# Attention with a mixture block on one core: the global attention's division, turning and value products rewritten, and the orders of all chunks replaced

## The chip, the core and the metric

The kernel runs on one core of a Trainium2 chip. The time is the device time of that core in microseconds (us). Three runs of the kernel before took 904.52, 904.91 and 905.95, a median of 904.91. The core's engines run side by side, each with its own queue of instructions: TensorE (PE) for matrix products, with its weight loads shown apart (PEld), VectorE (DVE), ScalarE (ACT), GpSimd (POOL), and SyncE (SP), which issues the DMAs. Instructions of different engines wait for each other by semaphores.

## The reference

Eight batches, eight heads, 512 local and 32 global tokens of 64 dimensions each. Global tokens attend to all 544 keys, local tokens to the 32 global keys and to a window of 32 keys on each side. The attention's rows then go through a normalised, gated pair of products (512 to 1536 to 512).

```
k_all = concat([k_g, k_l], axis=2); v_all = concat([v_g, v_l], axis=2)
out_g = sm(scale * q_g @ k_all.T) @ v_all            # 32 x 544 scores per head
s_ll  = where(|i - j| <= 32, scale * q_l @ k_l.T, -1e9)
out_l = sm(concat([scale * q_l @ k_g.T, s_ll])) @ v_all
x     = concat([out_g, out_l]) as (8 * 544) x 512    # B*S rows, H*D columns
xn    = x / sqrt(mean(x * x) + 1e-6) * rms_g
g, val = xn @ w_gate, xn @ w_val
out   = (g * sigmoid(g) * val) @ w_out
sm(s): e = exp(s - max(s)); e / (sum(e) + 1e-9)
```

The change concerns the line of `out_g`, and the order of everything that runs beside it.

## The kernel before

**Chunks.** The rows are worked in nine chunks. Chunks 0 to 7 are the 512 local tokens of one batch each, chunk 8 the 256 global tokens of all batches. A chunk is first attended (its scores, softmax and values), then normalised and split into f16 parts, and then sent through the gated products, which are most of PE's work: f16 products such as `pq<-xh,wt`, `pr<-wu,hs` and `po<-wo,h`. While the products of chunk c run, the attention of chunk c+1 and the first of chunk c+2 are done between them.

**Orders.** The function that builds the program records, for chunks 1 to 8, each step's instructions under a name. A table of names per chunk, `_ORDER_1` to `_ORDER_8`, then says in which order they are issued. All engines follow this order. Because the recorded calls are all played back in one place, nearly every instruction in the profile has the same line, L1929, and one tells them apart by their tiles. A name is a step and a part of it: `P5.0` and `R5.0` are the products of the fifth piece of work and what follows them on the other engines, `w`, `t`, `n` and `O` are weight fetches, the remainders of a piece of work, normalisation and output products. Names with a slash belong to attention: `S/0+1.0` is the step S (scores) of unit 0 of the next chunk, part 0. Chunk 0 is issued by another table that the change leaves as it is.

**Local attention.** A chunk from 2 to 7 has two local units (`local_halves`), of four heads each. Their steps are the loads L and V, scores S, the softmax in pieces M, N, E and F, the division D, the turn T on DVE (`STREAM_TRANSPOSE et<-e`: each 32x32 block is transposed in place), and the value products A and B (tile `a`), which add up 32 keys at a time, with the keys of four groups of 32 partitions. `A` holds the first part of the blocks and `B` the rest, so a unit's values are issued in one piece if B stands right behind A in the table, and in two otherwise. X and Y copy the result out of PSUM.

**Global attention.** `global_unit(b)` does the 32 global queries of batch b: eight heads as two halves h of four strips p of 32 partitions. There are eight such units; one falls into each of the tables 1 to 6 and two into table 7. Its steps:

- `GL`, `GV`: the loads of queries and keys (`gkq`, two tiles) and of the values (`gv`, three tiles). The values lie as five groups of 112 keys (the last of 96), the keys on the partitions.
- `GS`: sixteen score products into four PSUM banks.
- `GM`, `GN`: for each half the least score by DVE, the exponential with its sum by ACT, and, after the second, the sum's reciprocal on DVE.
- `GT` (`transp`): ten f32 transposes on PE into three PSUM banks (`gt`), and three copies by ACT to the tile `gpt`.
- `GA` (`values`): for each half, group of keys and strip one product, 40 in all, into one PSUM bank (`ga`). The turned exponentials (up to 112 keys x 32 queries) are the stationary side, 64 columns of values move.
- `GD` (`divide`): DVE multiplies the 128x128 result by the reciprocals (`gx`).
- `GX` (`turn`): one more f32 transpose on PE, and a copy by ACT into `xg`, where the global tokens of all batches gather for chunk 8.

**PSUM.** The four banks with the tag `pa`, given out in turn by `attn_bank`, serve the attention of both kinds: local scores and values, global scores, transposes and values, and some turns of the normalisation. A bank is free again when its last reader is done.

Of the kernel before, what the change touches and what calls it, by code (L numbers as in the profile page):

```python
# [9 lines left out]
F32 = mybir.dt.float32  # L10
# [12 lines left out]
P = 128  # L23
# [43 lines left out]
w1.0 w0.0 S/0+1.0 P8.0 P9.0 N1/0+1.0 N2/0+1.0 N0/0+1.0 N3/0+1.0 w2.0 M1/0+1.0 M2/0+1.0 E2/0+1.0 w3.0  # L67
M0/0+1.0 w5.0 P0.0 R9.0 F2/0+1.0 M3/0+1.0 R10.0 P4.0 P5.0 D2/0+1.0 w6.0 E3/0+1.0 F3/0+1.0 D3/0+1.0
D2/0+1.1 E0/0+1.0 F0/0+1.0 D3/0+1.1 D0/0+1.0 P1.0 R1.0 P10.0 T2/0+1.0 R2.0 GL/1+1.0 L/2+1.0 R5.0
R6.0 P6.0 P7.0 P11.0 D0/0+1.1 R7.0 E1/0+1.0 F1/0+1.0 D1/0+1.0 D1/0+1.1 P12.0 T3/0+1.0 T0/0+1.0 P2.0  # L70
P3.0 T1/0+1.0 w8.0 w9.0 A/0+1.0 B/0+1.0 X/0+1.0 R8.0 R11.0 P13.0 R12.0 R13.1 P16.0 R3.0 P14.0 P15.0
w12.0 w14.0 X/0+1.1 w15.0 R9.1 R4.0 V/2+1.0 R5.1 R13.0 R14.0 w42.0 Y/0+1.1 Y/0+1.0 w18.0 w20.0 R15.0
P24.0 P17.0 R17.0 R18.0 P25.0 R25.0 GS/1+1.0 P22.0 P23.0 GM/1+1.0 w21.0 w23.0 GM/1+1.1 GN/1+1.0
R26.0 w46.1 P26.0 P27.0 GN/1+1.1 GT/1+1.0 X/0+1.2 GT/1+1.1 R27.0 R28.0 w24.0 P20.0 R29.1 GT/1+1.2
GT/1+1.3 P21.0 R21.0 w26.0 R22.0 w17.0 P18.0 w27.0 GN/1+1.2 R16.0 R23.0 R24.0 P19.0 R25.1 R19.0
R20.0 S/2+1.0 M0/2+1.0 P32.0 M2/2+1.0 N3/2+1.0 GV/1+1.0 E2/2+1.0 M3/2+1.0 E3/2+1.0 N0/2+1.0 w48.1
M1/2+1.0 w44.0 N2/2+1.0 E1/2+1.0 w29.0 P33.0 R33.0 R34.0 N1/2+1.0 w30.0 R17.1 P28.0 P34.0 P35.0
# [12 lines left out]
R65.0 GX/1+1.0 R65.1 P57.0 n64.0 P58.0 P59.0 n61.0 D3/0+2.0 D3/0+2.1 n63.0 T1/0+2.0 w11.0 R59.0  # L90
R59.1 GX/1+1.1 n65.1 n66.0 T2/0+2.0 T0/0+2.0 T3/0+2.0 n65.0 n62.1 n63.1
# [16 lines left out]
T1/2+1.0 P41.0 F0/2+1.0 D0/2+1.0 R34.1 t36.0 GX/1+1.1 D2/2+1.1 T2/2+1.0 D0/2+1.1 t36.1 T0/2+1.0
R39.0 R40.0 t31.1 R41.0 t42.0 t37.1 A/2+1.0 B/2+1.0 X/2+1.0 Y/2+1.0 t37.0 X/2+1.1 Y/2+1.1 P50.0
# [2058 lines left out]
```

## Time and profile before

| | |
|---|---|
| median of three runs | 904.91 us |
| the profiled execution's own time | 906.6 us |
| its span in the trace | 904.8 us |
| MATMUL rows on PE, weight loads | 11430, 11430 |
| instructions on DVE, ACT, POOL | 1831, 1341, 244 |
| bytes moved by DMA | 212.03 MB in 101007 packets |

The profile is of one execution. Its span is the time from the first to the last instruction that it shows. Busy times are given by engine, and a group's row gives the number of instructions of one kind, their busy time and the mean time of one. PE's rows overlap, since a product streams in while the one ahead of it drains: what a product costs PE is read from the start of one row to the start of the next. An f32 product stands as two rows.

### The profile page before, as it was taken

The page shows a single profiled execution, that of the slowest core. Times are in us where ns is not written, and L with a number is a line of the kernel's source. Part 1 is how long each engine was busy: PE and PEld are TensorE (multiplying, and loading weights), DVE is VectorE, ACT ScalarE, POOL GpSimd, SP SyncE. Part 2 cuts the span into 40 slices and gives each one's busy share as a digit, 9 for nine tenths or more (in the row PEclk, how much of TensorE's full clock was granted, in tenths as well). Part 3 has the DMA queues.
Part 4 walks back from the last instruction along what each step waited for, and adds up shares of the span by engine and source line. Part 5 has one row for each costly group of instructions (what it writes and reads, how often), then busy time and mean ns, then how long its engine had stood idle before and what let it go on. Part 6 is the DMA issues. An engine that isn't in the chain of part 4 may idle for free. (4 is left out here: it accounts for less than half of the span.)

```text
span 904.8 us, 27760 instructions
## 1 busy us (share of the span) xinstructions
PE 867.7 (96%) x11430; PEld 667.4 (74%) x11430; DVE 725.8 (80%) x1831; ACT 555.3 (61%) x1341; POOL 277.2 (31%) x244
## 2 busy tenths in 40 slices
PE   6699979999999998999999999999999999999998
PEld 4544445545547885588888888888888888888887
DVE  6899998988787687878987888789877886787554
ACT  6899997547354666357665856668565852456232
POOL 0000000033335676515521344223521453134311
PEclk9699999999999999999999999999999999999999
DMA  9983625499277786698778777777876666888675
GB/s 331 406 288 126 196 69 171 153 290 305 75 216 254 224 266 205 195 318 248 222 268 272 247 225 254 267 234 252 282 244 206 227 206 211 261 245 274 218 244 181
DMA packets 101007, 212.03 MB, mean 234 GB/s; under 512 B 8081, under 2 KB 34449, under 8 KB 100881
## 3 DMA queue, kind: packets, MB, share of 16 engines
q1 hardware_dynamic: 100448, 209.94, 70.7%
q8 instruction: 89, 1.46, 0.7%
q10 hardware_dynamic: 432, 0.33, 0.1%
q14 instruction: 38, 0.30, 0.1%
HBM read 183.24 MB, written 27.00 MB: 232 GB/s over the span
## 5 line engine op out<-in xcount | busy, mean ns | idle before, releaser
L1929 PEld LDWEIGHTS <-wt 128*128 128x128 f16 x3312 | 321.6, 98 | 46.3 <-issue 7.0
L1929 PE MATMUL pq<-xh,wt 128*128 128x256 f16 x1152 | 204.0, 273 | 1.3 <-DVE s L1929 1.3
L1929 PE MATMUL pq<-ht,wt 128*128 128x256 f16 x1296 | 156.4, 273 | 1.9 <-DVE v L1929 1.3
L1929 PE MATMUL pq<-xl,wt 128*128 128x256 f16 x576 | 157.0, 273 | 0.0
L1929 ACT ACTIVATE e<-e,sm 128x128 f32<-128x128 f32 x288 | 104.3, 390 | 8.4 <-DVE sm L1929 8.4
L1929 POOL TENSOR_TENSOR e<-e,sm 128x512 f32<-128x512 f32 x24 | 29.2, 1225 | 217.2 <-DVE sm L1929 211.0
L1929 PE MATMUL pr<-wu,hs 128*128 128x256 f16 x792 | 92.6, 273 | 1.2 <-DMA wu<-wb 1.2
L1929 POOL TENSOR_TENSOR hs<-u,hs 128x512 f16<-128x512 f32 x50 | 61.1, 1236 | 97.1 <-ACT hs L1929 92.1
L1929 POOL TENSOR_TENSOR hu<-v,hu 128x256 f16<-128x256 f32 (+1 forms) x60 | 57.1, 966 | 106.3 <-ACT hu L1929 93.0
L1929 PEld LDWEIGHTS <-hs 128*128 128x128 f16 x792 | 77.3, 98 | 10.7 <-issue 1.8
L1929 PE MATMUL pr<-wu,hu 128*128 128x256 f16 x594 | 70.2, 273 | 0.6 <-ACT os L1929 0.6
L1929 ACT ACTIVATE t<-u,half_inv 128x512 f32<-128x512 f32 x72 | 50.3, 718 | 30.9 <-DVE u L1929 29.2
L1929 DVE TENSOR_TENSOR v<-pq,s 128x512 f32<-128x512 f32 x72 | 49.3, 685 | 20.3 <-PE pq L1929 17.4
L1929 PEld LDWEIGHTS <-hu 128*128 128x128 f16 x594 | 57.9, 98 | 7.6 <-issue 0.9
L1929 PE MATMUL po<-wo,h 128*128 128x512 f16 x288 | 63.6, 379 | 0.0
L1651 PE MATMUL p<-xh,wf 128*128 128x512 f16 x192 | 58.8, 379 | 3.4 <-DVE t L1763 1.5
L1929 DVE TENSOR_TENSOR s<-pq,s 128x512 f32<-128x512 f32 x66 | 44.5, 684 | 20.2 <-ACT s L1929 11.2
L1929 ACT COPY s<-pq 128x512 f32<-128x512 f32 x72 | 41.4, 582 | 30.7 <-PE pq L1929 22.2
L1929 DVE SCALAR_TENSOR_TENSOR t<-t,u 128x512 f32<-128x512 f32 x72 | 54.8, 768 | 5.1 <-ACT t L1929 4.9
L1929 PE MATMUL p<-xh,wf 128*128 128x512 f16 x192 | 58.6, 379 | 0.0
L1651 PEld LDWEIGHTS <-wf 128*128 128x128 f16 x288 | 27.7, 98 | 38.2 <-issue 4.4
L1929 ACT COPY u<-pq 128x512 f32<-128x512 f32 x36 | 21.0, 583 | 51.7 <-PE pq L1929 50.9
(380 smaller groups left out, 1704.3 us busy)
## 6 DMA issues: line engine op xcount, KB each, us to landing
wt<-wd SPq DMA_DIRECT2D x120, 512.0 KB, 5.8
wu<-wb SPq DMA_DIRECT2D x36, 512.0 KB, 5.9
wr<-in_w_in_dram SPq DMA_DIRECT2D x24, 512.0 KB, 8.9
wu<-wa SPq DMA_DIRECT2D x24, 512.0 KB, 4.6
k<-in_qkb_dram SPq DMA_DIRECT2D x24, 448.0 KB, 7.1
gkq<-in_gkq_dram SPq DMA_DIRECT2D x16, 576.0 KB, 7.5
wt<-wd SPq DMA_DIRECT2D x36, 256.0 KB, 4.4
v<-in_vb_dram SPq DMA_DIRECT2D x24, 352.0 KB, 5.6
```

The costliest lines, as they stand in the source:

```text
L1651: nc.tensor.matmul(ps[:, :n], rows[:, a, o : o + P], ch[z][k][:, :n], start=(k == 0 and i == 0), stop=(k == NK - 1 and i == 2),)
L1929: return lambda *a, **k: write(self.engine, lambda: call(*a, **k))
```

## The change

Four things are changed in the global unit, and all eight tables are replaced by others.

- **Division.** ACT multiplies the exponentials by the reciprocals, a half at a time (128x544), ahead of the turn. `GD` is gone.
- **Turning.** DVE transposes each half in 32x32 blocks (`STREAM_TRANSPOSE`, 128x544) into `gpt`. The ten PE transposes and ACT's three copies are gone.
- **Values.** The values lie in DRAM as 17 blocks of 32 keys, four strips of 32 partitions, 128 columns (two heads of 64). A product takes 32 keys on one strip: stationary are the 128 columns of v, and 64 columns move (32 queries of each half). 17 blocks by four strips are 68 products, and each strip has a PSUM bank of its own. The result is already turned, with the dimensions on the partitions; of its four quadrants the two on the diagonal are used (64x32 each). `gv` is loaded as two tiles, of nine and eight blocks.
- **Taking.** Eight copies of 64x32 bring the result from the four banks into `xg`, four on ACT and four on DVE. The PE transpose `gx` and the copy behind it are gone.

```diff
         def load_v(i):
             t = pool.tile([P, 1152], F32, tag="st", bufs=ST, name=f"gv{b}{i}")
-            n = min(1024, 5 * 512 - i * 1024)
-            nc.sync.dma_start(t[:GC, :n], gv[b, :, i * 1024 : i * 1024 + n])
-            st["v"] += [t[:, j * 512 : (j + 1) * 512] for j in range(n // 512)]
+            m0, n = ((0, 9), (9, 8))[i]
+            nc.sync.dma_start(t[:, : n * P], gv[b, :, m0 * P : (m0 + n) * P])
+            st["v"] += [t[:, m * P : (m + 1) * P] for m in range(n)]
...
-        def transp():
+        def turn():
             e = st["e"]
...
+            pt = pool.tile([P, 1280], F32, tag="gpt", bufs=1, name=f"gpt{b}")[:, : 2 * NG]
+            st["pt"] = pt.rearrange("p (h n) -> p h n", h=2)
             for h in range(2):
...
-                    nc.tensor.transpose(o, e[:, h, c * GC : c * GC + n], ident)
...
+                nc.scalar.mul(e[:, h, :], e[:, h, :], st["sm"][:, h, 3:4])
+            for h in range(2):
+                nc.vector.transpose(st["pt"][:, h, :], e[:, h, :])
 
         def values():
...
+            ps = st["a"] = [attn_bank(f"ga{b}{p}") for p in range(4)]
+            for m in range(NG // SG):
+                for p in range(4):
+                    r = slice(p * SG, (p + 1) * SG)
+                    nc.tensor.matmul(
+                        ps[p][:, : 2 * SG].rearrange("p (h q) -> p h q", h=2),
+                        st["v"][m][r, :],
+                        st["pt"][r, :, m * SG : (m + 1) * SG],
+                        start=(m == 0),
+                        stop=(m == NG // SG - 1),
+                        skip_group_check=True,
+                    )
+
+        def take():
+            for p in range(4):
+                for h in range(2):
+                    d = slice(h * D, (h + 1) * D)
+                    x, a = xg[d, p, b * SG : (b + 1) * SG], st["a"][p][d, h * SG : (h + 1) * SG]
+                    if p % 2 == 0:
+                        nc.scalar.copy(x, a)
+                    else:
+                        nc.vector.tensor_copy(x, a)
...
-            ("GV", lambda: [load_v(i) for i in (1, 2)], 0, [("GS", 1)]),
+            ("GV", lambda: load_v(1), 0, [("GS", 1)]),
...
-            ("GT", transp, 1, [("GN", GG[1] - 2)]),
-            ("GA", values, 1, [("GT", GG[2])]),
-            ("GD", divide, 0, [("GA", 1)]),
-            ("GX", turn, 1, [("GD", GG[3] - 1)]),
+            ("GT", turn, 0, [("GN", 1)]),
+            ("GA", values, 1, [("GT", GG[1] + GG[2] - 3)]),
+            ("GX", take, 0, [("GA", 1)]),
```

Of the tables, the first lines of `_ORDER_2`:

```diff
-P1.0 R1.0 P2.0 P4.0 R2.0 R4.0 w0.0 w4.0 GL/1+1.0 w2.0 P0.0 R0.0 R2.1 w4.1 w5.0 A/0+1.0 P3.0 P5.0
-R3.0 R5.0 R6.1 R6.0 P6.0 R6.2 t8.0 t9.0 t10.0 B/0+1.0 X/0+1.1 P7.0 R7.0 X/0+1.0 Y/0+1.1 P9.0 Y/0+1.0
+GL/1+1.0 w4.0 P0.0 R0.0 A/0+1.0 B/0+1.0 Y/0+1.1 X/0+1.0 P1.0 R1.0 w0.0 w2.0 w4.1 P2.0 P4.0 R4.0 R2.0
+P5.0 R2.1 L/2+1.0 R5.0 X/0+1.1 P7.0 R6.1 R6.0 t7.0 w5.0 P8.0 w9.0 R7.0 w11.1 Y/0+1.0 w13.1 w14.0
```

What this moves, at three places. The rows give the line, the operation, the tiles (out<-in, with the program's numbers) and the shape; L1929 of before is L1910 of after, and a LDWEIGHTS row is a weight load.

First PE, while the products of chunk 3 run, at the global unit of batch 2. Before, the ten transposes stand between two f16 products:

```order
L1929 MATMUL pq6_1_2610<-ht37_2564,wt3_13_2596 128x256
L1929 MATMUL gt20_2627<-ident_70,ge2_2600 112x128 x4
L1929 MATMUL gt2_2626<-ident_70,ge2_2600 96x128
L1929 MATMUL gt21_2628<-ident_70,ge2_2600 112x128 x4
L1929 MATMUL gt2_2626<-ident_70,ge2_2600 96x128
L1929 LDWEIGHTS wt3_20_2598
L1929 MATMUL pq6_2_2635<-ht36_2558,wt3_20_2598 128x256
```

and its values further on, as the first half's three rows, which the second half repeats:

```order
L1929 MATMUL pq6_3_2661<-ht37_2564,wt3_33_2652 128x256
L1929 MATMUL ga2_2638<-gv20_2585,gpt2_2625 32x64 x8
L1929 MATMUL ga2_2638<-gv21_2605,gpt2_2625 32x64 x8
L1929 MATMUL ga2_2638<-gv22_2606,gpt2_2625 32x64 x4
```

Now the transposes are gone, and the values are four banks in turn, 68 products in one go (the first round and the end of the last one):

```order
L1910 MATMUL pq5_4_2675<-xh35_2555,wt3_41_2651 128x256
L1910 MATMUL ga20_2628<-gpt2_2609,gv20_2579 128x64
L1910 MATMUL ga21_2629<-gpt2_2609,gv20_2579 128x64
L1910 MATMUL ga22_2630<-gpt2_2609,gv20_2579 128x64
L1910 MATMUL ga23_2631<-gpt2_2609,gv20_2579 128x64
L1910 MATMUL ga20_2628<-gpt2_2609,gv20_2579 128x64
```

```order
L1910 MATMUL ga22_2630<-gpt2_2609,gv21_2599 128x64
L1910 MATMUL ga23_2631<-gpt2_2609,gv21_2599 128x64
L1910 LDWEIGHTS wt3_41_2651
L1910 MATMUL pq6_4_2670<-ht37_2558,wt3_41_2651 128x256
```

The values stand a little later among the pieces of work than before (between the products of piece 41 of the chunk, against piece 33), and they write four banks where they wrote one.

Second DVE at the same unit. Before, the division of the result stood among the rows of the gated products (`u`, `v`) and the local turns (`et`):

```order
L1929 TENSOR_TENSOR u_4_2688<-pq5_4_2684,s6_4_2680 128x2x256
L1929 TENSOR_TENSOR gx2_2642<-ga2_2638,gsm2_2599 128x128
L1929 TENSOR_TENSOR v_4_2686<-pq6_4_2679,s1_4_2682 128x2x256
```

Now the turn of the exponentials stands well ahead of the values:

```order
L1910 RECIPROCAL sm9_2636<-sm9_2636 128x4
L1910 STREAM_TRANSPOSE gpt2_2609<-ge2_2594 128x544 x2
L1910 TENSOR_TENSOR v_3_2661<-pq6_3_2652,s1_3_2656 128x2x256
```

and the four copies of the result stand three rows behind the first of the piece of work (`s1_4`) whose products run right before the values on PE:

```order
L1910 TENSOR_TENSOR s1_4_2673<-pq5_4_2675,s1_4_2673 128x512
L1910 TENSOR_TENSOR s6_4_2671<-pq1_4_2672,s6_4_2671 128x512
L1910 STREAM_TRANSPOSE et90_2641<-e901_2660 128x512
L1910 COPY xg_77<-ga23_2631 64x32 x2
L1910 COPY xg_77<-ga21_2629 64x32 x2
L1910 SCALAR_TENSOR_TENSOR t6_2667<-t6_2667,u_3_2663 128x512
```

DVE's one row of 128x128 has become two turns ahead of PE's values and four small copies behind them.

Third PE, while the products of chunk 2 run, at the values of a local unit (tile `a7`). Before, they are one piece:

```order
L1929 MATMUL a73_2518<-et70_2470,v70_2441 64x96
L1929 MATMUL a73_2518<-et71_2471,v71_2442 64x96
L1929 MATMUL a70_2515<-et70_2470,v70_2441 64x96
L1929 MATMUL a70_2515<-et71_2471,v71_2442 64x96
```

Now the first part and the second are apart, with f16 products between them:

```order
L1910 MATMUL a73_2512<-et70_2465,v70_2438 64x96
L1910 MATMUL a73_2512<-et71_2466,v71_2439 64x96
L1910 LDWEIGHTS wt2_42_2475
L1910 MATMUL pq5_4_2494<-xh23_2386,wt2_42_2475 128x256
```

The same holds for three of the twelve units of chunks 2 to 7 more than before, as the tables have it.

More of the change, by code (lines that the diff above doesn't have):

```diff
@@ L72 @@
[L72 to L77, printed above, removed]
@@ new lines @@
+T0/0+1.0 P12.0 P13.0 T3/0+1.0 T2/0+1.0 R12.0 R13.1 R2.0 A/0+1.0 B/0+1.0 X/0+1.0 R3.0 R4.0 w12.0
+R13.0 R14.0 Y/0+1.1 w14.0 w15.0 X/0+1.1 P24.0 P25.0 R25.0 P26.0 P27.0 w18.0 Y/0+1.0 w20.0 P14.0
+P15.0 R26.0 R27.0 R28.0 P20.0 R5.1 GL/1+1.0 GS/1+1.0 w21.0 P16.0 GM/1+1.0 GN/1+1.0 w24.0 GM/1+1.1
+GN/1+1.1 GN/1+1.2 P18.0 S/2+1.0 M0/2+1.0 E0/2+1.0 R15.0 w11.0 M2/2+1.0 R29.1 P17.0 R17.0 P19.0
+M3/2+1.0 R18.0 R19.0 N3/2+1.0 GT/1+1.0 N1/2+1.0 GT/1+1.1 GV/1+1.0 w26.0 P21.0 R21.0 N2/2+1.0
+M1/2+1.0 R22.0 P22.0 P23.0 N0/2+1.0 P32.0 R20.0 R21.1 w27.0 E3/2+1.0 F3/2+1.0 R16.0 R17.1 F0/2+1.0
@@ L275 @@
+O14.0 O17.0 R50.3 O18.0 O19.0 O20.0 O21.0 O22.0 O23.0 w44.0 R56.0 O4.0 O7.0 O10.0 O13.0 O16.0 R56.1
+O24.0 w48.0 R50.1 O25.0 O26.0 O27.0 O28.0 O29.0 O30.0 O31.0 O32.0 R62.0 R56.2 O36.0 O37.0 O38.0
+O39.0 O40.0 O41.0 O33.0 O34.0 O35.0 R68.0 R68.1 R65.0 R59.0 R65.1
 """
@@ L968, in global_unit @@
         st = {}
-        sizes = [min(GC, NG - c * GC) for c in range(5)]
         def load():
@@ L1029, in softmax @@
                 nc.vector.reciprocal(sm[:, :, 3], sm[:, :, 3])
-        def transp():
+        def turn():
             e = st["e"]
-            pt = pool.tile([P, 2, 5, P], F32, tag="gpt", bufs=1, name=f"gpt{b}")
-            st["pt"] = pt
-            tail = attn_bank(f"gt{b}")
+            pt = pool.tile([P, 1280], F32, tag="gpt", bufs=1, name=f"gpt{b}")[:, : 2 * NG]
+            st["pt"] = pt.rearrange("p (h n) -> p h n", h=2)
             for h in range(2):
-                ps = attn_bank(f"gt{b}{h}")
-                for c, n in enumerate(sizes):
-                    o = ps[:n, c * P : (c + 1) * P] if c < 4 else tail[:n, h * P : (h + 1) * P]
-                    nc.tensor.transpose(o, e[:, h, c * GC : c * GC + n], ident)
-                nc.scalar.copy(
-                    pt[:GC, h, :4, :].rearrange("p c q -> p (c q)"), ps[:GC, :]
-                )
-            n = sizes[4]
-            nc.scalar.copy(
-                pt[:n, :, 4, :], tail[:n, : 2 * P].rearrange("p (h q) -> p h q", h=2)
-            )
@@ L1049, in values @@
-        def values():
-            ps = attn_bank(f"ga{b}")
-            for h in range(2):
-                for c, n in enumerate(sizes):
-                    for p in range(4):
-                        nc.tensor.matmul(
-                            ps[p * SG : (p + 1) * SG, h * D : (h + 1) * D],
-                            st["pt"][:n, h, c, p * SG : (p + 1) * SG],
-                            st["v"][c][:n, (2 * p + h) * D : (2 * p + h + 1) * D],
-                            start=(c == 0),
-                            stop=(c == 4),
-                        )
-            st["a"] = ps
@@ L1063, in divide @@
-        def divide():
-            ps = st["a"]
-            x = st["x"] = pool.tile([P, 512], F32, tag="w", bufs=3, name=f"gx{b}")[:, :P]
-            nc.vector.tensor_tensor(
-                x.rearrange("p (h d) -> p h d", h=2),
-                ps[:, :P].rearrange("p (h d) -> p h d", h=2),
-                st["sm"][:, :, 3].unsqueeze(2).to_broadcast([P, 2, D]),
-                ALU.mult,
-            )
-        def turn():
-            ps = attn_bank(f"gx{b}t")
-            nc.tensor.transpose(ps[:, :P], st["x"], ident)
-            nc.scalar.copy(
-                xg[:, :, b * SG : (b + 1) * SG], ps[:, :P].rearrange("p (k q) -> p k q", k=NK)
-            )
+                nc.scalar.mul(e[:, h, :], e[:, h, :], st["sm"][:, h, 3:4])
@@ L2066, in _layout @@
     gkq = gkq.reshape(B, 2, 2, P, SG + NG).transpose(0, 1, 3, 2, 4)
-    va = np.zeros((B, H, 5 * GC, D), f)
-    va[:, :, :SG] = v_g
-    va[:, :, SG:NG] = v_l
-    gv = va.reshape(B, H, 5, GC, D).transpose(0, 3, 2, 1, 4)
+    va = np.concatenate([v_g, v_l], 2).astype(f)
+    gv = va.reshape(B, 4, 2, NG // SG, SG, D).transpose(0, 1, 4, 3, 2, 5)
     def quarters(blocks, own):
```

370 lines of the change are left out of this document (183 added, 187 removed).

## The prediction

> **What bounds the kernel now.** I read the page first, then cores, busy time in stretches, waits of TensorE (PE), and for each product that goes or comes the timeline and its tile's rows.
>
> ```profile
> span 904.8 us, 27760 instructions
> PE 867.7 (96%) x11430; PEld 667.4 (74%) x11430; DVE 725.8 (80%) x1831; ACT 555.3 (61%) x1341; POOL 277.2 (31%) x244
> PE   6699979999999998999999999999999999999998
> core 0: 904.8 us, clock 0.991
> 463.00:562.00 99.00, 97.14 (x1473) 85.64 (x1471) 80.29 (x209) 62.39 (x160) 30.40 (x28) 1.00 0.79 250
> ```
>
> PE is busy for 96% of the span, at full clock, and from the eighth slice on it never rests for long. The last row is one stretch of 99 us in the middle: after its length come the busy times of PE, weight loads, DVE, ACT and POOL. PE has 97.1 of 99 us, DVE 80.3, ACT 62.4. So a microsecond of PE work there is a microsecond of the kernel, and DVE and ACT have some 19 and 37 us of room.
>
> What PE still waits for from 160 us on, where the orders that change apply:
>
> ```profile
> PE s L1929 <- issue: 1.6, 1, 1.6
> PE pq L1929 <- DVE v L1929: 1.3, 1, 1.3
> PE pq L1929 <- DVE s L1929: 1.3, 1, 1.3
> PE a L1929 <- issue: 1.2, 1, 1.2
> PE pr L1929 <- DMA wu<-wb: 1.2, 1, 1.2
> PE pq L1929 <- DMA wt<-wd: 0.6, 1, 0.6
> PE pr L1929 <- ACT os L1929: 0.6, 1, 0.6
> ```
>
> Seven waits, 7.8 us together: that is all that a better order can win.
>
> **What goes from PE, per global unit (eight units).** The timeline of PE (start, length, instruction) at one unit's values, at another's ten transposes, and at a last transpose:
>
> ```profile
> 231.51 0.38 PE L1929 MATMUL p<-xl,wf 128*128 128x512 f16 x1
> 231.73 0.38 PE L1929 MATMUL p<-xh,wf 128*128 128x512 f16 x1
> 232.04 1.33 PE L1929 MATMUL ga<-gv,gpt 112*32 112x64 f32 x80
> 233.30 0.39 PE L1929 MATMUL p<-xh,wf 128*128 128x512 f16 x1
> ...
> 401.60 1.26 PE L1929 MATMUL gt<-ident,ge 128*112 128x128 f32 x10
> 402.69 0.50 PE L1929 MATMUL pq<-ht,wt 128*128 128x256 f16 x3
> ...
> 332.56 0.27 PE L1929 MATMUL gx1t<-ident,gx 128*128 128x128 f32 x1
> 332.67 0.27 PE L1929 MATMUL pq<-xh,wt 128*128 128x256 f16 x1
> ```
>
> Lengths overlap, so I count from start to start. An f16 product of 512 columns takes 0.22 (231.51 to 231.73). From 231.73 to 233.30 are 1.57; without that product the values cost 1.35 us. The ten transposes cost 1.09 (401.60 to 402.69), the last one 0.11. Together **2.55 us per unit**, 20.4 in all.
>
> Two rates follow. Ten passes of 128 moving f32 columns in 1.09 us are 0.85 ns per column. And an f32 product is two matmul rows (40 products, 80 rows): two passes. The old values use four column strips side by side, so 80 passes are 20 rounds of 64 columns, 20 x 0.055 = 1.09 us; the other 0.26 is entering and leaving this form.
>
> **What comes to PE.** 17 blocks of 32 keys times 4 strips of 32 partitions are 68 products, 136 passes: 34 rounds of four strips. Each streams 64 columns, so streaming alone gives 34 x 0.055 + 0.26 = 2.11 us. But the stationary side is now 128 columns wide (two heads of v) instead of 32, and it is loaded anew for every pass. The nearest rows for such a load:
>
> ```profile
> L1929 PEld LDWEIGHTS ga<-gv,gpt x640: 106/110/113, 232.0 to 830.6; 112*32 112x32 f32 x128, 96*32 96x32 f32 x32
> L1929 PEld LDWEIGHTS a<-et,v x1920: 127/131/133, 187.7 to 731.2; 32*64 32x64 f32 x192
> L1929 PEld LDWEIGHTS ss<-nt,same x14: 190/190/192, 253.2 to 844.0; 128*128 128x128 f32 x14
> ...
> 253.38 0.29 PE L1929 MATMUL ss<-nt,same 128*128 128x16 f32 x2
> 253.52 0.59 PE L1929 MATMUL po<-wo,h 128*128 128x512 f16 x2
> ...
> 282.27 1.54 PE L1929 MATMUL a<-et,v 32*64 32x256 f32 x80
> 283.74 0.39 PE L1929 MATMUL pq<-ht,wt 128*128 128x256 f16 x2
> 287.78 1.14 PE L1929 MATMUL a<-et,v 32*64 32x96 f32 x80
> 288.86 0.39 PE L1929 MATMUL pq<-ht,wt 128*128 128x256 f16 x2
> 187.71 2.37 PE L1929 MATMUL a<-et,v 32*64 32x256 f32 x160
> 190.01 0.39 PE L1929 MATMUL p<-xh,wf 128*128 128x512 f16 x1
> ```
>
> A load row lasts 110, 131 and 190 ns for 32, 64 and 128 f32 columns: the latency is shared, the width is paid. The product `ss` streams 16 columns in two passes (0.014 each) and holds PE for 0.14 us, 253.38 to 253.52: the second pass's load lies open, **0.11 us for 128 columns**. That is one upper row. The lower: the second piece of a local unit's values (blocks 6, 7, 1, 8, 0, 9) gives each 32-partition strip 5 blocks x 2 passes, each with two loads of 64 columns, one for each head. It streams (96+96+64+64+32) x 2 x 0.85 = 0.60 us but takes 1.08, or 0.95 without 0.13 for leaving: 0.095 us for each 128 columns loaded in a strip. The same piece shows that the four strips load side by side: its 80 loads one after the other would take 80 x 0.055, over 4 us.
>
> So a round of the new product is set by its loads, between 0.095 and 0.11 us, and streaming (0.055) hides beneath. I take the middle, 0.104: 34 x 0.104 + 0.26 = 3.80 us, **1.25 more per unit, +10.0 in all** (ends: +7.5 and +11.6). Bounds from further off: streaming alone -0.44 per unit, -3.5; loads of the strips one after the other 136 x 0.11 = 15.0, +12.7 per unit, +101.
>
> The Trainium skill, "TensorE: Matmul & The Clock Gate", section "LDWEIGHTS (loading the stationary operand)", has a load take its columns over 1.2 in ns, whatever the number of rows. By it a round is an estimated 0.107 us and the sum would be +10.7; the load rows agree, 80 ns more for 96 more columns.
>
> **The order on PE.** Of the twelve units whose local values run in one or two pieces (A and B), one was in two pieces and four are now. Two pieces take 1.47 + 1.08 = 2.55 us against 2.30 in one, and one more entry, 0.09 (231.73 to 232.04 less 0.22): 0.34 each, three more, **+1.0**. The transposes entered without a gap, so their going saves nothing more.
>
> **ACT and DVE.**
>
> ```profile
> L1929 ACT COPY gpt<-gt x24: 367/577/591, 206.1 to 826.5; 112x512 f32<-112x512 f32 x16, 96x256 f32<-96x256 f32 x8
> L1929 ACT ACTIVATE ge<-ge,gsm x16: 732/743/751, 201.9 to 820.4; 128x544 f32<-128x544 f32 x16
> L1929 DVE STREAM_TRANSPOSE et<-e x48: 662/698/711, 181.1 to 726.8; 128x512 f32<-128x512 f32 x48
> L1929 DVE TENSOR_TENSOR gx<-ga,gsm x8: 254/288/292, 233.4 to 830.9; 128x128 f32<-128x128 f32 x8
> L1929 ACT COPY x<-a x24: 351/373/386, 190.2 to 737.5; 128x256 f32<-128x256 f32 x24
> L1929 DVE COPY x<-a x24: 406/416/426, 191.2 to 736.7; 128x256 f32<-128x256 f32 x24
> ```
>
> Per unit ACT loses three copies (2 x 0.58 + 0.37) and one small one; it gains two products of 544 columns, priced as the exponentials of that width, 2 x 0.74, and four copies of 64x32, at most 0.37 each. DVE loses 0.29; it gains two transposes of 544 columns, 2 x 0.698 x 544/512 = 1.48, and four copies, at most 0.42 each. That is at most +1.4 on ACT and +2.9 on DVE, in about 95 us: nothing, hidden by PE's queue of f16 products while DVE has 19 us free; all of it passed on would be 8 x 2.9 = 23. The loads of v fall from three to two per unit, 1120 to 1088 KB, with several products between load and use: nothing. GA now needs all four banks that the scores use. In chunk 1 only 42 products (42 x 0.22 = 9 us) lie between the local scores and GA, enough for the sixteen short reads; nothing.
>
> **Sum.** The profiled execution took 906.6 us with a span of 904.8; the three runs have a median of 904.91, so the span stands for the median. +10.0 + 1.0 + 0 (waits as many as now) = +11.0: **915.9 us**. Between the load rows, 913.4 to 917.5.
>
> **Rivals.**
> 1. *Loads hide (0.13).* If a strip's load runs wholly under the other strips' streams, a round is 0.055: -3.5 + 1.0, 902.4 us. It ends faster. Against it stands the second local piece, 0.95 instead of 0.60. The Trainium skill, same page, section "Part 3: Packing small matmuls — row/col tiling", tells of loads pulled ahead under matmuls of other row groups, a pack costing one matmul and a few ns per tile. By that rule this rival holds; the local piece does not bear it out for so few columns.
> 2. *The order pays (0.13).* The new tables remove all seven waits: 915.9 - 7.8 = 908.1. For it: two are waits for DVE sums, one for ACT and two for weights, all matters of place. Against: the same shared banks and queues remain.
> 3. *A wait takes the place (0.08).* DVE's copies of the result stand close behind GA: in the unit shown three rows of some 0.69 us lie between its last read of PE's product and them, 2.1 against 3.8 us of GA. DVE then waits up to 1.7, and its next sums free the banks of PE's next products. All passed on: 8 x 1.7 = 13.6, 929 us. DVE's free 19 us speak against it.
> 4. *Streaming does not hide under loads (0.05):* 0.16 per round, 5.7 us per unit, +25 in all, 931. *Strips load in turn (0.03):* near 1017.
>
> **Chances.** The forecast has 0.58. A difference of 0.2%, 1.8 us, is about what a measurement here can tell from none. Faster: rival 1 and a little of rival 2 and of the forecast's tail with fewer waits, 0.18. Within: the rest of rival 2's lower part and of that tail, 0.10. Slower: 0.72. The range takes in rival 1 and 2 and, above, the upper load price with some 4 us of new waits: 902 to 922; outside stay rivals 3 and 4 and tails. The likeliest case alone: 912 to 919.
>
> **What would show it.** Start to start over the 136 passes: 3.5 to 4.0 us, in rounds near 0.1, says loads; near 2.1 says rival 1; near 15 that strips load in turn. `gt` and `gx` transposes gone. The waits of PE after 160 us near 8 us. DVE's waits for `ga` above 1 us per unit with PE's waits for DVE grown would be rival 3. I am wrong if the GA burst is long and the span is not: then waits went that I took for fixed.

## The result, and the profile after

The changed kernel took 919.13 us, the median of four runs (918.18 to 919.32), against 905.23 us for the kernel before beside it. The ratio is 1.014, with a 95% interval of 1.0124 to 1.0156: slower by 13.9 us. The forecast was 915.9, between 902 and 922.

The page of the changed kernel (span, busy time of each engine) and its cores row:

```profile
span 916.4 us, 28522 instructions
PE 879.2 (96%) x11790; PEld 677.6 (74%) x11790; DVE 730.6 (80%) x1871; ACT 558.4 (61%) x1357; POOL 276.5 (30%) x244
```

```profile
core 0: 916.4 us, clock 0.993
```

PE has 11.5 us more, DVE 4.8, ACT 3.1. The profiled execution was the shortest of the four, and that of before, at 906.6 us, longer than all its timed runs, so the two spans lie only 11.6 apart. It is fairer to compare from the first instruction that the new tables order, the local scores `s` of the stretch of chunk 1. It starts at 168.80 us before and 167.12 after. Busy times in that one stretch (length; PE, weight loads, DVE, ACT, POOL; clock, DMA), before and then after:

```profile
168.80:904.80 736.00, 724.48 (x9729) 584.48 (x9728) 575.66 (x1407) 413.45 (x1035) 276.95 (x240) 1.00 0.74 238
```

```profile
167.10:916.40 749.30, 739.06 (x10089) 596.70 (x10088) 580.56 (x1447) 416.68 (x1051) 276.32 (x240) 1.00 0.71 234
```

The ordered part grew by 13.3 us at full clock, with PE's busy time. The timeline of PE at one unit's values, and the rows of the tile `ga` (minimum, median and maximum length in ns, first and last start), after:

```profile
319.06 0.27 PE L1910 MATMUL pq<-xl,wt 128*128 128x256 f16 x1
319.17 0.27 PE L1910 MATMUL pq<-xh,wt 128*128 128x256 f16 x1
319.37 4.02 PE L1910 MATMUL ga<-gpt,gv 32*128 32x64 f32 x136
323.32 0.61 PE L1910 MATMUL pq<-ht,wt 128*128 128x256 f16 x4
```

```profile
L1910 PEld LDWEIGHTS ga<-gpt,gv x1088: 181/187/187, 213.7 to 838.3; 32*128 32x128 f32 x182
L1910 PE MATMUL ga<-gpt,gv x1088: 270/270/318, 213.7 to 838.3; 32*128 32x64 f32 x182
...
  ACT xg L1910: 10.6, 4
  DVE xg L1910: 3.1, 2
```

From 319.17 to 323.32 are 4.15 us; without the f16 product ahead (0.11) the values cost 4.05. Before, values and transposes cost 2.55, and `gt` and `gx` are gone. The last two rows say who waited for `ga`: DVE's copies 3.1 us in two of the eight units, ACT's 10.6 in four. PE's waits from 160 us on, after:

```profile
PE pq L1910 <- DMA wt<-wd: 1.4, 1, 1.4
PE pr L1910 <- DMA wu<-wa: 1.3, 1, 1.3
PE pq L1910 <- DVE v L1910: 1.3, 2, 1.0
PE a L1910 <- issue: 0.7, 1, 0.7
PE s L1910 <- issue: 0.7, 1, 0.7
PE ga L1910 <- PE pq L1910: 0.3, 1, 0.3
PE pq L1910 <- ACT s L1910: 0.2, 1, 0.2
PE ga L1910 <- DVE gpt L1910: 0.2, 1, 0.2
```

6.1 us against 7.8 before. For the accounts below I added PE's steps, each from the start of one row to the start of the next, from that first `s` to the end of the span; a "gap" is what a step lasts beyond its product's streaming, where that is over 0.15 us. The names of the last columns are those of the experiments.

| us on PE | before | after | e5 | e6 | e7 | e11 |
|---|---|---|---|---|---|---|
| f16 products of the other work | 641.4 | 641.5 | 643.3 | 648.8 | 642.4 | 641.5 |
| global values (and transposes) | 19.8 | 31.6 | 31.6 | 36.1 | 31.7 | 5.2 |
| local values `a` | 28.1 | 28.8 | 28.8 | 28.2 | 27.8 | 29.2 |
| gaps | 11.6 | 12.0 | 12.3 | 26.5 | 17.9 | 27.1 |
| scores, the rest and the tail | 35.2 | 35.5 | 35.1 | 35.0 | 35.1 | 36.3 |
| sum | 736.0 | 749.3 | 751.0 | 774.5 | 754.9 | 739.2 |

Of 13.3 us, 11.9 are the global values (eight entries of 0.09, before and after, stand in the first line), 0.7 the local values in more pieces, 0.3 gaps.

### The profile page after: what moved, and what is told of

Same layout as the page of the kernel before. It is cut to its first block, busy times and chain, and to the rows that moved or that the text cites. A ratio compares the mean times of both kernels' runs of the same rounds, so it can differ in the third digit from the quotient of the medians.

```text
span 916.4 us, 28522 instructions
## 1 busy us (share of the span) xinstructions
PE 879.2 (96%) x11790; PEld 677.6 (74%) x11790; DVE 730.6 (80%) x1871; ACT 558.4 (61%) x1357; POOL 276.5 (30%) x244
## 4 chain that ended last, share of the span: by engine, by line
PE 78%; DVE 6%; ACT 2%; DMA 2%; issue 1%; POOL 1%; DVEq 0%; ACTq 0%; POOLq 0%
PE pq L1910 32%; PE pr L1910 14%; PE p L1910 10%; PE po L1910 7%; PE ga L1910 3%; PE po L1775 3%; PE a L1910 3%; PE s L1910 2%; DMA wt<-wd 1%; PE gs L1910 1%; ACT wq L508 1%; DVE x L1910 1%; DVE s L1910 1%; ACT s L1910 1%; DMA wu<-wa 0%
## 5 line engine op out<-in xcount | busy, mean ns | idle before, releaser
L1910 PEld LDWEIGHTS <-wt 128*128 128x128 f16 x3312 | 321.7, 98 | 48.1 <-issue 7.0
L1910 PE MATMUL pq<-xh,wt 128*128 128x256 f16 x1152 | 203.8, 273 | 0.4 <-ACT s L1910 0.2
L1910 PE MATMUL pq<-ht,wt 128*128 128x256 f16 x1296 | 155.8, 273 | 3.0 <-DMA wt<-wd 1.4
L1910 PE MATMUL pq<-xl,wt 128*128 128x256 f16 x576 | 157.0, 273 | 0.0
L1910 ACT ACTIVATE e<-e,sm 128x128 f32<-128x128 f32 x288 | 104.3, 390 | 29.0 <-DVE sm L1910 28.9
L1910 POOL TENSOR_TENSOR hu<-v,hu 128x512 f16<-128x512 f32 (+1 forms) x60 | 59.2, 1000 | 148.2 <-ACT hu L1910 139.2
L1910 PE MATMUL pr<-wu,hs 128*128 128x256 f16 x792 | 93.5, 273 | 0.0
L1910 POOL TENSOR_TENSOR e<-e,sm 128x512 f32<-128x512 f32 x24 | 25.6, 1080 | 206.1 <-DVE sm L1910 206.1
L1910 POOL TENSOR_TENSOR hs<-u,hs 128x512 f16<-128x512 f32 x50 | 60.0, 1212 | 83.9 <-ACT hs L1910 70.6
L1910 PEld LDWEIGHTS <-hs 128*128 128x128 f16 x792 | 77.2, 98 | 9.4 <-POOL hs L1910 0.3
L1910 PE MATMUL pr<-wu,hu 128*128 128x256 f16 x594 | 71.4, 273 | 1.3 <-DMA wu<-wa 1.3
L1910 ACT COPY s<-pq 128x512 f32<-128x512 f32 x72 | 41.7, 582 | 46.9 <-PE pq L1910 28.7
L1910 ACT ACTIVATE t<-u,half_inv 128x512 f32<-128x512 f32 x72 | 50.2, 718 | 27.5 <-DVE u L1910 25.4
L1910 DVE TENSOR_TENSOR v<-pq,s 128x512 f32<-128x512 f32 x72 | 49.1, 684 | 19.8 <-PE pq L1910 15.5
L1910 PEld LDWEIGHTS <-hu 128*128 128x128 f16 x594 | 57.6, 98 | 8.8 <-issue 2.1
L1910 PE MATMUL po<-wo,h 128*128 128x512 f16 x288 | 63.9, 379 | 0.0
L1910 DVE TENSOR_TENSOR s<-pq,s 128x512 f32<-128x512 f32 x66 | 44.9, 686 | 21.7 <-ACT s L1910 16.9
L1910 DVE SCALAR_TENSOR_TENSOR t<-t,u 128x512 f32<-128x512 f32 x72 | 52.7, 740 | 9.5 <-ACT t L1910 9.2
L1910 PE MATMUL p<-xh,wf 128*128 128x512 f16 x192 | 58.6, 379 | 0.0
L1632 PEld LDWEIGHTS <-wf 128*128 128x128 f16 x288 | 27.7, 98 | 37.1 <-issue 3.2
L1910 PEld LDWEIGHTS <-wf 128*128 128x128 f16 x288 | 27.6, 98 | 33.6 <-issue 0.8
```

The source lines that it names most:

```text
L1632: nc.tensor.matmul(ps[:, :n], rows[:, a, o : o + P], ch[z][k][:, :n], start=(k == 0 and i == 0), stop=(k == NK - 1 and i == 2),)
L1910: return lambda *a, **k: write(self.engine, lambda: call(*a, **k))
```

## The experiments

They ran on several chips, each time with the kernel before beside them (medians of 905.75 to 907.42), and ratios are to that.

### What sets the 4 us: two runs with half a side

**e1_move32**: half the moving columns.

```diff
-                        ps[p][:, : 2 * SG].rearrange("p (h q) -> p h q", h=2),
+                        ps[p][:, :SG],
                         st["v"][m][r, :],
-                        st["pt"][r, :, m * SG : (m + 1) * SG],
+                        st["pt"][r, 0, m * SG : (m + 1) * SG],
```

> Each of the 68 value products moves 32 columns (the first half's queries) instead of 64, so the second head's result is not computed; the 128 stationary columns are as in the change. Theory (a round of four strips is set by loading 128 columns in each strip): the values still take 3.9 to 4.0 us from start to start. Rival (the strips run two at a time, so that a round is two streams of 64 columns, 2 x 0.055 = 0.11, which gives the same 0.111 us): half the stream, some 2.1 us per unit and 8 x 1.85 = 15 us off the span.

Where PE's clock was full, the values took 3.93 us from start to start instead of 3.96, in five units of eight. The rival fell: halving the stream changes 0.03 us. The time was 931.9 (one run), and that is another matter: in three units the values took 4.6 to 5.0. Timeline of PE there, and busy times around it (the number after POOL's is the granted clock):

```profile
427.00 4.70 PE L1910 MATMUL ga<-gpt,gv 32*128 32x32 f32 x136
431.63 1.67 PE L1910 MATMUL pq<-ht,wt 128*128 128x256 f16 x7
```

```profile
427.00:429.00 2.00, 2.00 (x73) 2.00 (x72) 1.57 (x4) 1.13 (x3) 2.00 (x2) 1.00 0.69 254
...
430.10:436.90 6.80, 6.80 (x58) 5.21 (x55) 3.51 (x8) 1.60 (x4) 4.86 (x5) 0.50 0.23 77
436.90:440.00 3.10, 3.10 (x31) 2.74 (x29) 1.23 (x2) 1.29 (x4) 0.00 (x0) 0.99 0.21 37
```

The clock fell to half in the middle of the values, without a wait, and stayed there for 6.8 us. Why in these three units and not in the other five, no run shows.

**e2_hold64**: half the stationary columns.

```diff
+                    d = slice(m % 2 * D, (m % 2 + 1) * D)
-                        ps[p][:, : 2 * SG].rearrange("p (h q) -> p h q", h=2),
-                        st["v"][m][r, :],
+                        ps[p][d, : 2 * SG].rearrange("p (h q) -> p h q", h=2),
+                        st["v"][m][r, d],
```

> Each of the 68 value products holds 64 stationary columns, one head's values, the first head for even blocks and the second for odd ones, so that each head's result lacks half its keys; 64 columns move as in the change. Theory (loads of 128 columns set the round): half the load, a round near 0.055, the values at 2.0 to 2.3 us per unit, some 14 us off the span. Rival (streams of two strips in turn): 3.9 to 4.0 us, no change.

The timeline of PE at one unit, e2:

```profile
422.21 0.27 PE L1911 MATMUL pq<-xh,wt 128*128 128x256 f16 x1
422.41 1.66 PE L1911 MATMUL ga<-gpt,gv 32*64 32x64 f32 x136
424.00 0.61 PE L1911 MATMUL pq<-ht,wt 128*128 128x256 f16 x4
```

1.59 us from start to start, a round of 1.44/34 = 0.042 us, less than the 0.055 that I had taken for 64 moving columns. So the stationary side sets the round, as the theory has it, but not in proportion: 0.110 for 128 columns, 0.042 for 64 of alternating halves. How much of that is the width, and how much that two halves can work side by side, e2 does not part; e4 below shows that the width is not the whole of it. The time was 909.1 (one run), some 10 us below the changed kernel, where the values alone fell by 8 x 2.36 = 19: half of it was given back.

### Twice as many products: gaps without a semaphore

**e3_perhead** and **e4_swap** both make 136 products of a unit's 68. e4 is shown for the pace of its rows alone, not as a form to use.

```diff
+                    for h in range(2):
+                        d = slice(h * D, (h + 1) * D)
-                        st["v"][m][r, :],
-                        st["pt"][r, :, m * SG : (m + 1) * SG],
+                            st["v"][m][r, d],                          # e3
+                            st["pt"][r, h, m * SG : (m + 1) * SG],
+                            st["pt"][r, h, m * SG : (m + 1) * SG],     # e4
+                            st["v"][m][r, h * D : (h + 1) * D],
```

> 136 products: for each head its 64 columns of v as the stationary side and its own 32 queries moving, so that the two unused quadrants are not computed. A strip still loads 128 columns per block and pass, 64 for each head. Theory (a strip's loads go one after the other, whatever they are cut into): the values stay at 3.8 to 4.1 us, time 919 within 2. Rival (the two halves of the columns load side by side): a round near 0.055, 2.1 us, time near 904.

> The sides swapped: stationary are the 32 queries of one head (32 columns), moving that head's 64 columns of values; 136 products, so a strip loads 2 x 32 = 64 columns per block and pass instead of 128. The result is not turned by this, so 16 turns of 32x32 on VectorE take the place of the eight copies. Theory (loads per strip set the round): 2.0 to 2.3 us of values per unit, 8 x 1.8 = 14 us off, time near 905 if VectorE hides its 16 turns. Rival (streams of one strip in turn, 2 x 0.055 for the two heads): values near 4.0, time 919.

954.2 us (ratio 1.0539, 1.0499 to 1.0580) and 959.4 (1.0609, 1.0574 to 1.0643): all expectations missed. The timeline of e3 at one unit, with the idle time ahead in brackets, and the clock behind it:

```profile
326.44 2.62 PE L1912 MATMUL ga<-gpt,gv 32*64 32x32 f32 x242
331.58 0.46 PE L1912 MATMUL ga<-gpt,gv 32*64 32x32 f32 x30 [2.52 <-issue]
```

```profile
332.00:335.40 3.40, 3.40 (x22) 2.43 (x18) 3.13 (x8) 1.04 (x4) 0.00 (x0) 0.51 0.11 42
```

The products themselves are quick: 242 rows in 2.6 us. But inside every unit stands one gap of 2.1 to 5.4 us for which the trace shows no semaphore ("issue"), and behind most of them the clock is at half for 3.4 us or more. A new theory: PE runs out of fetched instructions in a long row of tiny ones.

The pace of e4's rows, at the same unit:

```profile
323.91 2.60 PE L1911 MATMUL ga<-gv,gpt 32*32 32x64 f32 x242
```

That is e3's pace, with half its stationary columns and twice its moving ones: from start to start e3 and e4 take 10 ns per row (one pass of a product), e2 takes 10.7, the change 27.8. So in these three forms, with 64 or 32 columns on either side, the widths do not set the pace; what does stays open.

**e8_two_pieces** parts these rows.

```diff
-            ("GA", values, 1, [("GT", GG[1] + GG[2] - 3)]),
-            ("GX", take, 0, [("GA", 1)]),
+            ("GA", lambda: values(range(9)), 1, [("GT", GG[1] + GG[2] - 3)]),
+            ("GB", lambda: values(range(9, 17)), 0, [("GA", 0)]),
+            ("GX", take, 0, [("GB", 1)]),
```

> The 136 products for each head apart (64 stationary columns, 32 moving), in two pieces with some four pieces of f16 work between them. In one piece these 272 rows held one gap of 2.3 to 5.4 us in each unit, without a semaphore, after 160 to 240 rows; without it the rows take about 0.01 us each. Theory (PE runs out of fetched instructions in a long row of tiny ones, and the gap and the half clock behind it go with the length): no gap, two pieces of 1.4 to 1.7 us, 3.1 us per unit instead of 4.05, time 910 to 914. Rival (the gap belongs to these tiles or to a place in the program): the gaps stay, time above 930.

930.6 us (ratio 1.0269, 1.0234 to 1.0304). The pieces without a gap took 1.45 and 1.27 us from first to last row, 2.72 for the 272 rows against 3.75 for the 136 of the change. But three of the sixteen pieces held gaps of 0.5 to 2.1 us, and PE's waits put down to issue were 11.5 us in all, in local values and f16 products too. So the gap goes with the length in most places, not in all. The time is 24 us less than e3's, but still 9 above the change and where the rival had it: the theory was half right at most.

### The order: the change again, old orders, joined pieces

These two and e8 ran on one chip with **e5_again**, the unchanged copy of the changed kernel.

> The changed kernel itself, timed beside the next three for a base on the same chip: 12 to 14 us over the kernel before, the values 3.95 us from start to start in each of the eight units.

921.1 us, ratio 1.0154 (1.0133 to 1.0176), as expected.

**e6_old_orders**. The tables are those of before; shown is one table's piece:

```diff
-GM/1+1.1 GN/1+1.1 t8.1 P9.0 GN/1+1.2 P10.0 ... t10.3 GT/1+1.0 GT/1+1.2 R13.2 t9.1 t14.0 t15.0 GT/1+1.1
+GM/1+1.1 GN/1+1.1 t8.1 P9.0 P10.0 ... t10.3 R13.2 t9.1 t14.0 t15.0 GN/1+1.2 GT/1+1.0
-... t31.3 GD/1+1.0 R31.0 ... GX/1+1.0 GX/1+1.1
+... t31.3 GX/1+1.0 GX/1+1.1 GX/1+1.2 GX/1+1.3 R31.0 ...
```

> The new global unit under the old orders: the tables of before, in which the unit's softmax end, division and turn stand where the ten transposes stood, the values where they stood (in the first table behind the local softmax reads that hold the banks), and the eight takes where the division stood. Theory (the unit's own products cost 8 x 1.5 = 12 us, the order about 1): 917 to 921, the values 3.95 us per unit, PE's other waits from 160 us on 6 to 10 us. Rival (the new orders cost or win several us): more than 3 us below or above the changed kernel.

946.2 us (ratio 1.0437, 1.0419 to 1.0455), 25 above e5: my theory fell. PE's waits from 160 us on, the largest, e6:

```profile
PE ga L1911 <- DVE gpt L1911: 6.1, 2, 3.8
PE pq L1911 <- ACT s L1911: 2.7, 2, 2.3
PE pq L1911 <- issue: 2.4, 2, 2.2
```

By the table of steps, gaps cost 14.2 us more than in e5; the global values 4.5 more and the f16 products 5.5 more, at the same counts, since the clock is lower (0.973 over the span, against 0.989). So the new tables are no small term beside the new unit: in the places that the old ones give it, the unit makes PE wait for DVE's turn of the exponentials, and waits cost a second time through the clock. How much of it is due to where I put its steps in the old tables stays open.

**e7_joined**: in four units the token of the second piece is moved to the first.

```diff
-A/2+1.0 t42.1 t37.2 O1.0 P41.0 R41.2 t43.1 t33.0 B/2+1.0
+A/2+1.0 B/2+1.0 t42.1 t37.2 O1.0 P41.0 R41.2 t43.1 t33.0
```

> The changed kernel with the second piece of a local unit's values put right behind the first in the four units where the new tables part them. Theory: 4 x 0.34 = 1.4 us below the changed kernel where the waits stay (one of the four was parted before the change too). Rival (the parting avoids waits): not below it.

926.5 us (ratio 1.0203, 1.0179 to 1.0227), 5.4 above e5: the rival held. The local values took 0.94 us less, 0.24 for each unit joined, where I had reckoned 0.34, but the gaps grew by 5.6. One of them, timeline of PE, e7:

```profile
649.13 2.28 PE L1910 MATMUL a<-et,v 32*64 32x256 f32 x149
653.81 0.45 PE L1910 MATMUL a<-et,v 32*64 32x32 f32 x11 [2.40 <-issue]
```

In these tables, parting a unit's 160 rows is worth more than it costs. The gap shown is like e3's, and the waits put down to issue rose from 0.8 us in e5 to 3.8; the rest of the 5.6 are waits for weights and for ACT, which was not traced further.

### Taking the cost away: f16 values

**e9_half** computes the global values in f16, one pass instead of two.

```diff
-                nc.scalar.mul(e[:, h, :], e[:, h, :], st["sm"][:, h, 3:4])
+                nc.scalar.mul(ps[:, h, :], e[:, h, :], st["sm"][:, h, 3:4])   # ps, pt in f16
...
+        def narrow():
+            w, i = st["raw"].bitcast(F16), 0
+            for t in st["vt"]:
+                n = t.shape[1]
+                nc.scalar.copy(w[:, i : i + n], t)
```

> The changed kernel with the divided exponentials and the values in f16 (ACT casts both tiles of v, 1152 and 1024 columns, into the tile that held the exponentials): 68 products of one pass instead of two, 128 f16 columns stationary, 64 moving. This rounds the global rows' probabilities and values to f16, so it computes the same thing less exactly. Theory (a round of four strips is set by its loads): 17 rounds of at most 0.109 us, the f16 products' own pace beside a load of 128 columns, so 1.7 to 2.1 us per unit instead of 4.05, 8 x 2.0 = 16 us below the changed kernel, near 905 on the first chip's scale, and near or below the kernel before; ACT's casts, 8 x 2.3 us, are hidden. Rival (the waits decide, as with the old orders and the joined pieces): the values fall to about 2 us, and the time falls by less than 8 us.

917.4 us, ratio 1.0127 (1.0102 to 1.0151). The values took 0.52 us from first to last row in five of the eight units, 0.65 to the next product where nothing waited: a round of 0.031, far under the 0.109 that I had allowed. That is 26 us less on PE, and the time fell by 2 to 4 us (the ratio from e5's 1.0154 to 1.0127, with intervals that overlap): the rival. Where it went, timeline of ACT at one unit, and PE's waits, e9:

```profile
627.03 2.10 ACT L1920 CAST ge<-gv 128x1152 f16<-128x1152 f32 x2
629.03 2.45 ACT L1920 ACTIVATE e<-e,sm 128x128 f32<-128x128 f32 x8
631.38 0.57 ACT L1920 COPY s<-pq 128x512 f32<-128x512 f32 x1
```

```profile
PE a L1920 <- issue: 5.6, 3, 2.5
PE pq L1920 <- ACT u L1920: 4.9, 3, 2.6
PE pq L1920 <- ACT s L1920: 3.7, 4, 2.5
PE ga L1920 <- ACT ge L1920: 2.1, 3, 1.4
```

ACT's casts, and the exponentials that queue behind them, hold up its copies `s<-pq`, which free PE's banks: 8.6 us of waits for `u` and `s`.

**e10_pool** cuts the casts into four and gives them to POOL.

```diff
-                nc.scalar.copy(w[:, i : i + n], t)
+            nc.gpsimd.tensor_copy(w[:, m0 * P : (m0 + n) * P], st["vt"][i // 2][:, o * P : (o + n) * P])
```

> The f16 form of the run before, with the casts of v taken from ACT to POOL, which is 30% busy, and cut into four pieces of 512 or 640 columns spread over the stretch between the turn and the values (in the sixth table the values stand some three pieces of work later). Theory (in the run before, the values fell by 3.3 us per unit, 26 us in all, and ACT's two casts of 1.1 us in a row gave most of it back as waits of PE for ACT): the waits for ACT fall from 10.7 us to under 3, the time to 895 to 908, below the kernel before. Rival (the new orders are fitted to the 4 us of the values, and whatever shortens them makes other waits): the waits stay above 20 us, time 910 or more.

921.3 us, ratio 1.0179 (1.0151 to 1.0206). The waits for ACT fell to 1.0 us, but PE now waited 8.7 us for POOL's casts and 4.9 for weights. The rival again. The timeline of POOL ahead of a late cast, e10:

```profile
431.09 1.16 POOL L1920 TENSOR_TENSOR hs<-u,hs 128x512 f16<-128x512 f32 x1 [4.01 <-ACT hs L1920]
432.19 1.12 POOL L1920 CAST ge<-gv 128x512 f16<-128x512 f32 x1
```

The cast itself is short; it stood in POOL's queue behind a row that waited 4 us for ACT.

**e11_cast_load** lets the load itself cast, and keeps the changed kernel's tables.

```diff
-            t = pool.tile([P, 1152], F32, tag="st", bufs=ST, name=f"gv{b}{i}")
-            nc.sync.dma_start(t[:, : n * P], gv[b, :, m0 * P : (m0 + n) * P])
+            t = pool.tile([P, 1152], F32, tag="st", bufs=ST, name=f"gv{b}{i}").bitcast(F16)
+            nc.gpsimd.dma_start(t[:, : n * P], gv[b, :, m0 * P : (m0 + n) * P])
```

> The f16 form again, with no cast on any engine: both tiles of v are loaded by POOL's queue straight into f16 where the second tile's load stood (GV), and the tables are the changed kernel's own, word for word. Theory (the f16 values take 0.65 to 0.75 us per unit as in the two runs before, 26 us less PE work than in the changed kernel, and what gave that back were the casts' places on ACT and POOL): no waits of the values for ACT or POOL, waits of PE from 160 us on 8 to 15 us, time 893 to 905, below the kernel before. Rival (the new orders hold only for a unit with 4 us of values): other waits of 15 to 25 us take the place, time 910 or more, as in both runs before.

911.65 us, ratio 1.0059 (1.0036 to 1.0082): the best of the changed versions that compute the whole result, and still above the kernel before, as the rival had it, though its global values take 0.65 us where before took 2.46. PE's largest waits, e11:

```profile
PE a L1909 <- issue: 5.8, 3, 3.0
PE pq L1909 <- ACT u L1909: 2.2, 2, 1.7
PE pq L1909 <- ACT s L1909: 2.1, 5, 0.7
PE pq L1909 <- DMA wt<-wd: 1.8, 2, 1.6
PE pq L1909 <- issue: 1.6, 2, 1.0
PE s L1909 <- issue: 1.1, 1, 1.1
```

By the steps, 26.4 us went from the values and 15.1 came back as gaps. No cast waits are left among them; what is largest is issue, 8.5 us.

**e12_shift** asks about those. I numbered PE's rows, loads, products and its 81 to 91 semaphore and drain rows together, from the program's start, and listed the gaps over 0.7 us inside runs of small products from 165 us on. An excerpt, from my own count (run, number of the last product ahead of the gap, its rest by 256, its start in us, tile):

```
before        8128  192  345.34  a          e3_perhead    8128  192  328.84  ga
before        8384  192  349.98  s          e3_perhead   14528  192  541.25  ga
after        10944  192  439.46  a          e8           24256  192  849.58  ga
e7_joined    17087  191  651.23  a          e11          13504  192  540.93  a
```

In the fourteen traces, 46 of 48 such gaps stand at rest 191 or 192. The experiment adds 48 rows ahead of everything:

```diff
+        for _ in range(12):
+            nc.tensor.matmul(gp[0][:1, 2 * P : 2 * P + 2], g2[:, 0:1], ident[:, :2], start=True, stop=True)
```

> The kernel of the run before with twelve tiny f32 products of two columns added near 18 us, whose result nothing reads: 48 more rows of loads and products on PE ahead of everything else, and nothing moved. Theory (in all runs so far the waits of PE put down to issue inside runs of small products stand at a row whose number among PE's loads and products is 192 over a multiple of 256, and only where the 256 rows up to there took less than about 2.4 us: PE fetches its instructions in blocks of 256, and waits where it has used a block up faster than the next arrives): the same rows of the program stand 48 numbers later, so the gaps of 1.4 to 3.2 us at the four places of the run before go, at most two others come (in the local values near 282 and 648 us), each still at a number of 192 over a multiple of 256; the waits for issue fall from 8.5 to under 4 us, and the time by 3 to 7 us, to 904 to 909. Rival (the gaps belong to these products, their banks or their place): they stay at the same products, waits for issue 7 to 10 us, time 910 to 914.

916.3 us, ratio 1.0094 (1.0062 to 1.0126). The same burst of local values in the timelines of e11 and then of e12:

```profile
538.61 2.54 PE L1909 MATMUL a<-et,v 32*64 32x256 f32 x140
542.34 0.42 PE L1909 MATMUL a<-et,v 32*64 32x64 f32 x20 [1.20 <-issue]
```

```profile
543.62 2.23 PE L1911 MATMUL a<-et,v 32*64 32x256 f32 x116
547.22 0.71 PE L1911 MATMUL a<-et,v 32*64 32x64 f32 x44 [1.37 <-issue]
```

The gap moved from behind the 140th to behind the 116th product, 24 products and 24 loads earlier in the program, and so kept its number, 13504. Three other gaps of e11, two of them among f16 products, kept the number of the row ahead of them too (5312, 6336 and 10944), with other instructions standing there. Two more of e11's went and three new ones came, all with a row of rest 192 ahead. The place theory holds: the gaps belong to the number, not to the product. The price theory does not: waits for issue were 11.9 us instead of 8.5, gaps came where the 256 rows ahead had taken 2.7 and 3.5 us, and the time rose by 3 to 5 us (by the ratios, by the medians; the intervals of the two ratios overlap). A fixed limit of 2.4 us doesn't tell which block is late.

## Why the prediction came out as it did

- **PE is the bound.** Right: +13.3 us in the ordered part, with PE's busy time +14.6 at clock 1.00. DVE and ACT gained 4.9 and 3.2 us there, hidden as forecast.
- **What goes, 2.55 per unit.** Right; `gt` and `gx` are gone.
- **What comes, 3.80 per unit.** The mechanism was right (e1, e2), the size not: 4.05, so +12.0 instead of +10.0. The step that was off is "I take the middle, 0.104" (the middle of 0.095 and 0.11 is 0.1025): the round is 3.75/34 = 0.110, the upper row. The lower row, 0.095 from the local values, was of another kind. There a strip loads twice 64 columns, and e8 shows that 2 x 64 columns take 2.72/34 = 0.080 where 128 in one load take 0.110. The piece's 80 passes in 0.95 us are 12 ns each, near the 10 ns that e3 and e4 keep with 64 and with 32 columns, so 0.095 was hardly a price of width at all. The Trainium skill's section "LDWEIGHTS (loading the stationary operand)" of "TensorE: Matmul & The Clock Gate" gave an estimated 0.107, and the trace agrees within 3%.
- **The pieces, +1.0.** 0.7 for three. That they cost anything on balance was wrong in these tables: e7, without them and without the parting that before had, is 5.4 us slower.
- **Waits as many as now.** 6.1 against 7.8: right in sum, but for no good reason. No row showed that the new tables keep the waits low; under the old orders the same unit has 14.2 us more of gaps (e6), so that the order cost no more than it did was luck as far as the forecast goes. And I counted the waits put down to issue, 2.8 of the 7.8 us, as matters of place among tiles and banks; both stand at row 192 of a block (8128 and 8384).
- **"The span stands for the median".** This was the weak end of the sum. The profiled execution of before was 1.4 us above the later median, 905.23, and its start 1.7 us later than that of the profile after. Of the 3 us that the forecast lacks, 2.0 are the values; the rest is of the size of such differences between runs and was not traced further.
- **Rivals.** *Loads hide* fell: 3.96 us, not 2.1. So the rule weighed there (the Trainium skill, same page, "Part 3: Packing small matmuls — row/col tiling") does not hold for four f32 loads of 128 columns; with f16, where the round is 0.031 and 64 columns stream in 0.027, it nearly does. *The order pays*: the waits that it removes beside the old kernel are 1.7 us, not 7.8; beside the old orders with the new unit (e6) they are many times that. *A wait takes the place*: DVE waited 3.1 us for `ga` in all, and PE's waits for DVE did not grow. *Streaming does not hide* and *strips in turn* fell with e1 and with the 3.96 us. The latter's "near 1017" was also summed wrongly: the +101 stands in place of the +10, which gives some 1007.

One remark on the part about the change: the numbers 33 and 41 in the weight tiles' names there are a group and a part of it, not pieces of work.

## What to carry to other kernels

Before cutting a product's depth to 32 keys, count the stationary columns that each strip loads: here 68 loads of 128 f32 columns in two passes cost 4.05 us per unit where transposes and deep products cost 2.55, and neither fewer moving columns nor side-by-side strips hide it. In a kernel whose engine of the bound is 96% busy under a fixed order, an edit's own cost is only half the account: 26 us taken from PE won between nothing and 9 here; the rest came back as waits at other places (15.1 us of gaps in e11). That the order was fitted to the longer unit is the likely reason, but no run fitted it anew. Parting long rows of tiny products by large ones paid here twice, 24 us in e8 and 5 in e7's four units. And since gaps of 1 to 3 us move with the number of rows ahead of them, a difference of a few us between two versions can be that alone.

## What the runs showed of the hardware

- **PE's gaps without a semaphore stand at one place of each 256 rows.** 46 of 48 gaps of 0.7 to 5.4 us inside runs of small products stand there, and with 48 rows more ahead of everything four gaps kept their row numbers while other instructions stood at them. That instructions arrive in such blocks is the reading that fits; no row of a trace shows a fetch. The Trainium skill, "Runtime: NRT & Kernel Launch", section "Instruction fetch mechanics", tells of a refill in blocks of 256 instructions, mostly hidden; the block agrees, "hidden" does not where 256 rows take 1.3 us (e3).
- **PE's clock falls to half in spells of 3.4 us and multiples,** in e3 behind gaps of 2.5 us, and in e1, in three units of eight, in values without any gap that moved half as many columns. In e5 a spell came right behind one wait of 2.6 us for weights (timeline and busy times below), but behind one of 2.8 us in e12, also for weights, the clock stayed at 1.00 from 623.2 to 630 us; what decides between the two is not shown.

```profile
460.07 0.82 PE L1910 MATMUL pr<-wu,hu 128*128 128x256 f16 x6 [2.61 <-DMA wu<-wa]
```

```profile
461.10:464.50 3.40, 3.40 (x19) 2.42 (x17) 1.40 (x2) 0.36 (x1) 2.83 (x3) 0.50 1.02 379
```

- **An f16 load of 128 columns is far cheaper than an f32 one**: rounds of 0.031 and 0.110 us. The Trainium skill, "TensorE: Matmul & The Clock Gate", section "Weight-path perf modes — Fast Weight Load (FWL) and DoubleRow", has that such a load is read faster when it has 128 columns and isn't f32, which agrees.
- **Small f32 products with at most 64 columns on either side kept one pace,** 10 to 11 ns a pass: 10.7 with 64 columns held and 64 moved (e2), 10.0 with 64 and 32 (e3), 9.9 with 32 and 64 (e4).
